# Two attention layers on one core: the last output block multiplied bank by bank, its last 72 rows prepared sooner

## The chip, the cores and the metric

The kernel runs on one core of a Trainium2 chip. The time is device microseconds of one execution. A core has a matrix engine (TensorE, PE in the profile, with its weight loads as PEld), three engines for element-wise work (VectorE or DVE, ScalarE or ACT, GpSimd or POOL), and SyncE (SP), which here issues nearly all of the transfers between DRAM and on-chip memory. On-chip memory is SBUF; the matrix engine writes into PSUM, eight banks of 128 partitions by 512 floats.

## The reference, cut to what matters

Two attention layers, A and B, work on two inputs of 2048 rows by 576 columns with 32 heads of 18. Their outputs stand side by side in the result. Only A matters for the change:

```python
q = (x @ wq).reshape(B, S, H, Dh).transpose(0, 2, 1, 3)   # 32 heads of 18
k = x @ wk                                                # one head, shared
v = x @ wv
p = softmax(einsum("bhqd,bkd->bhqk", q, k) * Dh ** -0.5)
o = einsum("bhqk,bkd->bhqd", p, v)
out_A = o.transpose(0, 2, 1, 3).reshape(B, S, H * Dh) @ wo
```

B is a causal attention in four segments with a memory that is carried from segment to segment. The last lines of the work, and the whole change, belong to the product with `wo` of A.

## The kernel before, in words

The 2048 rows of each layer are worked in four chunks (`c`) of 512 columns of a transposed layout: heads and their 18 features lie on partitions, rows of x lie along the free axis. A block is (layer, chunk, group of four heads); the list `blocks` mixes those of A and B, and the last one is chunk 3 of A, head group `hg` 7. Blocks are cut into turns `k` of three score tiles. In each turn of the main loop (L1130) the kernel writes the scores for this turn (PE), their exponentials (ACT, some by DVE), and the products with the values for the turn two before (`products`, L919). The engines PE, ACT and DVE run their instructions in the order in which the program writes them. SP and POOL get an order from a scheduler, which works from dependencies and its own cost estimates; the order of the text is only one input of that.

When a group of four heads is done, `products` copies its accumulator `O` to `oe` on DVE (L945) and stores it to the DRAM tensor `oA` (L947). Row 0 of each head's 19 rows is the sum of the softmax, rows 1 to 18 are the head's output. So the division comes later, in `finish` (L1005), as steps that are put into a list by `at` with a turn at which they are due, and taken from it by `due`:

- `begin` loads the sums from `oA` into `sm` (L674);
- `inv` takes the reciprocal on DVE (L688), stores it to `rA` (L695), and asks for the heads;
- `load` reads the heads' rows from `oA` into the tile `xh` (L702), 126 rows (seven heads) for each of t = 0 to 3, and 72 rows (four heads) for t = 4;
- `weights` reads the reciprocals, spread over the rows, into `rb` (L709);
- `heads` multiplies `xh` by `rb` on POOL (L723), which is called weighing.

Head group 6 of a chunk releases t = 0 to 3, head group 7 releases t = 4. For the last chunk the reciprocal of group 7 is due five turns after its `begin`.

Most chunks are multiplied with `wo` in the shade of later attention work, by `out_proj` (L752), which `run_fill` (L822) takes piece by piece into each turn. Two chunks are left for the end: chunks 2 and 3 of A, called `rows`. Their product is made differently: each operand is split into two float32r parts, a rounded one (`hi`, a copy on ACT, L1080) and the rest (`lo`, a subtraction on DVE, L1081). `halve_w(t)` does this for `wo`, `halve_heads(key, t)` for the heads. For t = 0 to 3 three matmuls then make one product. For t = 4 the 72 rows are repeated on more partitions with three transfers inside SBUF (`repeat`, L1108 to L1110), so that two matmuls do it; the halves of t = 4 are made by two casts on ACT (L1099) and two operations on DVE (L1100). `multiply` (L1198) runs over the eight PSUM banks for one t: four blocks of 128 output rows by two halves of 288 columns.

The end (from L1215) is written in this order: for chunk 2 the halves of t = 0 to 4 of weights and heads; then for chunk 3 the halves of t = 0 to 3, each after its weighing; then for each of the two chunks five calls of `multiply`, t by t over all eight banks, and four times two evictions (one on ACT, one on DVE, L1248) and a store of 128 rows (L750). For chunk 3, the transfers of `repeat` and the halves of t = 4 come just before the fifth `multiply`.

Of the kernel before, what the change touches and what calls it, by code (L numbers as in the profile page):

```python
# [8 lines left out]
F32 = mybir.dt.float32  # L9
F32R = mybir.dt.float32r  # L10
# [10 lines left out]
S, D, H, DH = 2048, 576, 32, 18  # L21
NSEG, L = 4, 512
C = 512
NCH = S // C
# [9 lines left out]
PBUFS = 9  # L34
# [43 lines left out]
def attention_pair_kernel(ctx, tc, a_xT, a_w, a_wo, b_xT, b_w, b_wo, b_beta, ident_d, hmask_d, bmask_d, cmask_d, sel_d, zmask_d, selx_d, sely_d, out):  # L78
# [840 lines left out]
    def products(b, m, hf):  # L919


        ab, c, hg = b
        if m == hf == 0:
            acc[0] = psO.tile([128, C], F32, name="O")
        o = acc[0]
        last = (NKT - 1 if ab == "A" else 2) == m
        for j in range(4):
            kt = turn_of(c, hg)[j // 2][m] if ab == "A" else m
            p = state[b + (kt,), j // 2]
            assert all(x[3] is not p for x in slow)  # L930
# [5 lines left out]
            nc.tensor.matmul(  # L936
                o[32 * j : 32 * j + 32, q0 : q0 + n],
                v,
                p[:, j % 2, p0 : p0 + n],
                start=m == hf == 0,  # L940
                stop=last and hf == 1,
            )
        if last and hf:
            osb = pa.tile([128, C], F32, name="oe", bufs=4)
            nc.vector.tensor_copy(osb, o)  # L945
            od = oA if ab == "A" else oB
            nc.sync.dma_start(od[c][4 * hg : 4 * hg + 4].rearrange("h r t -> (h r) t"), osb)  # L947
            return hg
        return None

# [29 lines left out]
    next(memory)  # L980
    prefetch("A", 2)
    FILL = 60
    later, weighed, loaded, summing = [], {}, [0], set()
# [21 lines left out]
    def finish(k, ab, c, hg):  # L1005

        ts = range(4) if hg == 6 else range(4, 5)
        lo, hi = (0, 28) if hg == 6 else (28, 32)
        box, need = {}, 3 if ab == "B" and c > 0 else 1
        weighed.setdefault((ab, c), 0)  # L1010
        last = (ab, c) == blocks[-1][:2]

        d0, d1, d2, d3 = (0, 2 if hg == 6 else 5, 0, 3) if last else (2, 5, 3, 5) if (ab, c) == ("B", 0) else (2, 4 if ab == "B" and hg == 6 else 5, 3, 6)

        def begin(k):
            assert ab == "A" or c not in LATE_ASK or asked[0] >= c
            summing.add(hg)
            box[0] = sums(ab, c, lo, hi)
            at(k + d1, 0, lambda: True, inv)

        def inv(k, part=0, of=1 if last or hg == 7 else 4 if ab == "B" and c else 2):
            inverses(ab, c, lo, hi, box[0], part, of)
            if part < of - 1:
                at(k + 1, 0, lambda: True, lambda k: inv(k, part + 1, of))
                return
            summing.remove(hg)
            for t in ts:
                at(k, 0, place, lambda k, t=t: load(k, t))
# [12 lines left out]

        def weights(k, t):
            loaded[0] += need
            tiles = load_inverses(ab, c, t)
            box[t, t] = weigh(ab, c, t, tiles)
            at(k + d3, 1, lambda: True, lambda k: heads(k, t))

        def heads(k, t):
            box[t, t].pop(0)()
            if box[t, t]:  # L1050
                at(k, 1, lambda: True, lambda k: heads(k, t))
                return
# [14 lines left out]
    with tc.manual_schedule(engines={ENG.PE, ENG.Activation, ENG.DVE}):  # L1067
# [59 lines left out]
            nc.vector.tensor_reduce(fms[0:1, 1:2], pf[0:1, 0:128], axis=AX.X, op=ALU.max)  # L1127

        wparts = []
        for k in range(len(turns) + 2):  # L1130
            now[0] = k
            exps = [scores(its[n], pr, i == 1) for i, (n, pr) in enumerate(turns[k])] if k < len(turns) else []
# [16 lines left out]
            ends = k > 1 and any(hf and its[n][3] == (NKT - 1 if its[n][0] == "A" else 2) for n, hf in prods[k - 2])  # L1149
            if slow and (slow[0][0] <= k or not ends):  # L1150
# [30 lines left out]
                fill.pop(0)  # L1181
            k += 1

        rows = [key for key, steps in fill] + [blocks[-1][:2]]
        assert len(rows) == 2 and all(ab == "A" for ab, c in rows)
        halves_of = {}

        def halve_heads(key, t):
            R = RT[t]
            x = halves_of[key, t] = pp.tile([128, 2, 512], F32R, name="P", bufs=PBUFS)  # L1190
            if t < 4:
                halve(x[:R, 0], x[:R, 1], parts[key][:R, t])
                return
            hi = pp.tile([128, 2, 512], F32R, name="PD", bufs=2)
            mixed(x[:, 0], hi[:, 0], parts[key][:, 4], some[:, 0:1])
            mixed(x[:88, 1], hi[:88, 1], raws[key], some[:88, 1:2])

        def multiply(key, t, dst):  # L1198
            R = RT[t]
            x = halves_of[key, t]  # L1200
            for g in range(8):
                i, c0 = g // 2, 288 * (g % 2)
                for m, (xp, wp) in enumerate(((0, 0), (1, 0), (0, 1)) if t < 4 else ((0, 0), (1, 1))):
                    if t == 4:
                        R = (128, 88)[m]
                    nc.tensor.matmul(
                        dst[g],
                        x[:R, xp, 128 * i : 128 * i + 128],
                        wparts[wp][:R, t, c0 : c0 + 288],
                        start=t == m == 0,  # L1210
                        stop=t == 4 and m == 1,
                    )


        repeat(rows[0])  # L1215
        for t in range(5):
            if t:
                halve_w(t)
            due(k, 4)
            k += 1  # L1220
            halve_heads(rows[0], t)
        for t in range(4):
            while weighed[rows[1]] <= t:
                due(k, 4)
                k += 1
            halve_heads(rows[1], t)
        for n, key in enumerate(rows):
            end = key == rows[-1]
            banks = [psE.tile([128, 2, 512], F32, name="E") for _ in range(3)]
            dst = [bk[:, hf, :288] for bk in banks for hf in range(2)]  # L1230
            dst += [psO.tile([128, C], F32, name=nm)[:, :288] for nm in ("O", "F")]
            for t in range(5):
                while end and weighed[key] <= t:
                    due(k, 4)
                    k += 1
                if end and t == 4:
                    repeat(key)
                    halve_heads(key, t)
                multiply(key, t, dst)
            for i in range(4):  # L1240
                if end:
                    osb = pp.tile([128, 2, 512], F32, name="P", bufs=PBUFS)[:, :, :288]
                elif i < 2:
                    osb = pp.tile([128, 2, 512], F32, name="W", bufs=2)[:, :, :288]
                else:
                    osb = pa.tile([128, D], F32, name="osb", bufs=2).rearrange("p (f n) -> p f n", f=2)
                for hf in range(2):
                    (nc.vector.tensor_copy if hf else nc.scalar.copy)(osb[:, hf], dst[2 * i + hf])  # L1248
                out_store(*key, i, osb)
        assert not later  # L1250
    attention.close()

# [226 lines left out]
```

## Time and profile before

| what | value |
|---|---|
| median of three runs | 1404.8 us (1403.82 to 1405.02) |
| the profiled execution's own time | 1405.02 us |
| its span, first to last instruction | 1403.3 us |
| PE busy | 1383.7 us, 99% of the span |
| ACT busy | 1199.0 us, 85% |
| DVE busy | 1048.5 us, 75% |
| POOL busy | 233.2 us, 17% |
| DMA moved | 173.67 MB, mean 124 GB/s |

The span is what the profile shows of the execution; the time of a run is a little longer, since it holds what lies around the program. Rows of a timeline begin with the start in us from the start of the span and the length; then engine, line of the kernel, operation, tile written and tiles read, sizes, and count; an idle time before it stands in brackets with what ended it. Where SP carries a q (SPq), the row is the issuing of a transfer, not the transfer itself. The length of several merged instructions reaches from the first start to the last end.

### The profile page before, as it was taken

What the parts mean: (1) busy time and instruction counts of PE and PEld (TensorE: products, weight loads), DVE (VectorE), ACT (ScalarE), POOL (GpSimd) and SP (SyncE); (2) the same over time, 40 slices, a digit from 0 to 9 for tenths busy, and PEclk for the clock granted to TensorE, in tenths of its full rate; (3) what the DMA queues carried; (4) which work ended last, traced back from release to release, by engine and by line L of the source; (5) the groups of instructions that cost most, each with busy time, mean ns of one, the idle gap of its engine ahead of it and who ended that gap; (6) DMA issues with size and microseconds to landing.
All of it is one profiled execution on the core that took longest, in us unless ns stands there. A gap on an engine that the chain in (4) does not pass through costs nothing.

```text
span 1403.3 us, 41194 instructions
## 1 busy us (share of the span) xinstructions
PE 1383.7 (99%) x17452; PEld 836.5 (60%) x17452; DVE 1048.5 (75%) x1565; ACT 1199.0 (85%) x1484; POOL 233.2 (17%) x342
## 2 busy tenths in 40 slices
PE   9999999999999999999999999999999999999997
PEld 6787888755554555555555555555555555555557
DVE  6656466477787788787888877876878778887884
ACT  4543434489999999999999999999999999999991
POOL 2442000003312211412110122113010220001002
PEclk9999999999999999999999999999999999999999
DMA  9866546577465445332312442232103221110023
GB/s 273 264 213 188 160 144 227 177 221 217 141 192 168 137 144 165 99 116 78 112 59 71 144 155 60 86 118 80 52 34 102 100 76 47 35 61 21 18 83 112
DMA packets 91288, 173.67 MB, mean 124 GB/s; under 512 B 14702, under 2 KB 23015, under 8 KB 90668
## 3 DMA queue, kind: packets, MB, share of 16 engines
q1 hardware_dynamic: 84968, 161.24, 36.8%
q0 software_dynamic: 1664, 4.78, 1.3%
q10 hardware_dynamic: 4464, 4.93, 1.0%
q8 instruction: 139, 2.28, 0.7%
q14 instruction: 53, 0.43, 0.1%
HBM read 99.65 MB, written 70.67 MB: 121 GB/s over the span
## 4 chain that ended last, share of the span: by engine, by line


## 5 line engine op out<-in xcount | busy, mean ns | idle before, releaser
L906 ACT ACTIVATE P<-E 128x1024 f32<-128x1024 f32 (+1 forms) x800 | 787.5, 1075 | 2.1 <-PE E L888 1.6
L903 DVE COPY W<-E 128x1024 f32<-128x1024 f32 (+2 forms) x416 | 453.3, 1090 | 142.9 <-PE E L888 80.5
L936 PE MATMUL O<-P,VA 128*32 128x256 f32 x7504 | 507.1, 379 | 0.0
L906 ACT ACTIVATE P<-W 128x1024 f32<-128x1024 f32 (+1 forms) x330 | 370.0, 1121 | 6.3 <-DVE W L903 5.7
L936 PEld LDWEIGHTS O<-P,VA 128*32 128x32 f32 x7504 | 259.1, 110 | 137.7 <-issue 4.3
L888 PE MATMUL E<-xl,kstA 56*128 56x512 f32 x1920 | 317.3, 430 | 2.0 <-ACT P L906 1.8
L888 PEld LDWEIGHTS E<-xl,kstA 56*128 56x128 f32 x1920 | 155.0, 184 | 159.1 <-issue 96.1
L911 POOL TENSOR_SCALAR_AFFINE_SELECT P<-P 128x256 f32<-128x256 f32 (+1 forms) x192 | 94.6, 493 | 410.0 <-ACT P L906 401.4
L723 POOL TENSOR_TENSOR xh<-xh,rb 126x512 f32<-126x512 f32 (+1 forms) x55 | 70.7, 1308 | 432.7 <-DVE PD L869 185.0
L739 PE MATMUL F<-woB,xh 126*32 126x192 f32 (+1 forms) x1920 | 126.5, 338 | 0.0
L936 PE MATMUL O<-PD,VA 128*32 128x256 f32 x688 | 88.9, 379 | 0.0
L739 PEld LDWEIGHTS F<-woB,xh 126*32 126x32 f32 (+1 forms) x1920 | 38.6, 108 | 74.8 <-issue 68.7
L936 PE MATMUL O<-P,vseg 128*32 128x256 f32 (+2 forms) x1536 | 81.5, 344 | 0.1
L945 DVE COPY oe<-O 128x512 f32<-128x512 f32 x64 | 44.3, 692 | 42.8 <-PE O L936 42.5
L862 DVE TENSOR_SCALAR PD<-E 128x512 uint32<-128x512 f32 x86 | 59.2, 688 | 17.8 <-PE E L888 16.1
L259 PE MATMUL pj<-xh,wBh 128*126 128x512 f32 x180 | 72.1, 400 | 0.0
L259 PE MATMUL pj<-xh,wBl 128*126 128x512 f32 x180 | 71.6, 398 | 0.0
L124 ACT CAST qp<-pj 126x512 fp32r<-126x512 f32 (+1 forms) x54 | 30.8, 583 | 39.3 <-DVE kmB L454 22.4
L739 PE MATMUL F<-woA,xh 126*32 126x192 f32 (+1 forms) x960 | 63.9, 338 | 0.0
L896 PE MATMUL E<-stB 56*128 56x256 f32 (+3 forms) x512 | 61.4, 348 | 2.0 <-ACT P L906 1.5
L936 PEld LDWEIGHTS O<-P,vseg 128*32 128x32 f32 x1536 | 48.8, 109 | 24.4 <-issue 1.8
L125 DVE TENSOR_TENSOR qp<-pj,qp 126x512 fp32r<-126x512 f32 (+1 forms) x54 | 36.7, 685 | 35.6 <-ACT qp L124 35.6
(222 smaller groups left out, 1556.5 us busy)
## 6 DMA issues: line engine op xcount, KB each, us to landing
stB<-kB SPq DMA_DIRECT2D x96, 144.0 KB
stB<-qB SPq DMA_DIRECT2D x32, 288.0 KB
xl<-qA SPq DMA_DIRECT2D x30, 288.0 KB
oA<-oe SPq DMA_DIRECT2D x32, 256.0 KB
oB<-oe SPq DMA_DIRECT2D x32, 256.0 KB
qA<-qp SPq DMA_DIRECT2D x16, 504.0 KB
kB<-qp SPq DMA_DIRECT2D x16, 504.0 KB
qB<-qp SPq DMA_DIRECT2D x16, 504.0 KB
```

The lines of the kernel that those rows point to most:

```text
L125: hold(nc.vector.tensor_tensor(qp[:R, 1, :n], src, qp[:R, 0, :n].bitcast(F32), op=ALU.subtract))
L259: nc.tensor.matmul(dst, w[:, c0 : c0 + M], x, start=i == 0, stop=i == len(ops) - 1)
L723: ins = tc.keep_in_program_order(nc.gpsimd.tensor_tensor(dst, a, b, op=op))
L739: nc.tensor.matmul(dst[32 * j : 32 * j + 32], parts[ab, c][: RT[t], t, r0 : r0 + 32], wo[ab][: RT[t], t, c0 : c0 + n], start=start, stop=stop,
L862: v.tensor_scalar(y, e, EXP_A, EXP_B, op0=ALU.mult, op1=ALU.add)
L888: nc.tensor.matmul(e[:, j], kstA[rows, 128 * kt : 128 * kt + 128], st[rows, h, :], start=True, stop=True)
L896: nc.tensor.matmul(e[:, j, c0 : c0 + 512 - 128 * k], st[rows, 4 + h, ks], st[rows, h, 128 * k :], start=True, stop=True)
L903: gate.append(nc.vector.tensor_copy(src[:, hs, :n], e[:, hs, :n]))
L906: nc.scalar.activation(p[:, hs, :n], src[:, hs, :n], AF.Exp, scale=SCALE)
L911: nc.gpsimd.affine_select(diag, diag, pattern=[[0, 2], [0, m], [1, 128]], base=0, channel_multiplier=-1, compare_op=ALU.is_ge, fill=0.0)
L936: nc.tensor.matmul(o[32 * j : 32 * j + 32, q0 : q0 + n], v, p[:, j % 2, p0 : p0 + n], start=m == hf == 0, stop=last and hf == 1,)
L945: nc.vector.tensor_copy(osb, o)
```

## The change

Four things are done.

1. The store of `oe` of the very last block goes to ScalarE's DMA queue instead of SP's.
2. For the last chunk's head group 7, `inv` (reciprocal, store of `rA`, and then the load of the 72 rows, the read of `rb` and the weighing) isn't put into the list with a due turn, but held, and written right behind the halves of t = 3 of chunk 2. `repeat` for chunk 3 is written right after its weighing, ahead of all multiplications.
3. Chunk 2's halves of the heads for t = 0 and of the weights for t = 1 are written in the last turn of the main loop, on both sides of the last piece of `out_proj`, so ahead of the last `oe` copy.
4. The last chunk is multiplied bank by bank: for each of the eight banks all five t, then its eviction; a store follows each pair of banks, and the last 128 rows are stored in two halves. Its t = 4 halves are written behind chunk 2's evictions.

```diff
@@ products
-            nc.sync.dma_start(od[c][4 * hg : 4 * hg + 4].rearrange("h r t -> (h r) t"), osb)
+            queue = nc.scalar if b == blocks[-1] else nc.sync
+            queue.dma_start(od[c][4 * hg : 4 * hg + 4].rearrange("h r t -> (h r) t"), osb)
@@ finish, begin
-            at(k + d1, 0, lambda: True, inv)
+            if last and hg == 7:
+                held.append(inv)
+            else:
+                at(k + d1, 0, lambda: True, inv)
@@ main loop
+        first, second = ("A", NCH - 2), ("A", NCH - 1)
...
+            if k > len(turns):
+                halve_heads(first, 0)
             if memory is None:
                 whole = run_fill()
...
+            if k > len(turns):
+                halve_w(1)
@@ the end
-        repeat(rows[0])
+        repeat(first)
         for t in range(5):
-            if t:
+            if t > 1:
                 halve_w(t)
             due(k, 4)
             k += 1
-            halve_heads(rows[0], t)
+            if t:
+                halve_heads(first, t)
+            if t == 3:
+                held.pop()(k)
         for t in range(4):
-            while weighed[rows[1]] <= t:
+            while weighed[second] <= t:
                 due(k, 4)
                 k += 1
-            halve_heads(rows[1], t)
...
+            halve_heads(second, t)
+        while weighed[second] <= 4:
+            due(k, 4)
+            k += 1
+        repeat(second)
...
+        dst = eight_banks()
+        for t in range(5):
+            multiply(first, t, dst)
...
+        halve_heads(second, 4)
+        dst = eight_banks()
+        for i in range(4):
+            osb = pp.tile([128, 2, 512], F32, name="P", bufs=PBUFS)[:, :, :288]
+            for hf in range(2):
+                for t in range(5):
+                    multiply(second, t, dst, [2 * i + hf])
+                evict(osb, hf, dst[2 * i + hf])
+                if i == 3:
+                    r0 = second[1] * C + 128 * i
+                    nc.sync.dma_start(out[r0 : r0 + 128, 288 * hf : 288 * hf + 288], osb[:, hf])
+            if i < 3:
+                out_store(*second, i, osb)
```

`multiply` takes the banks as an argument (`gs`, all eight by default). `evict` is the copy of L1248, on DVE for the second bank of a pair and on ACT for the first; `eight_banks` names the same eight banks as before.

More of the change, by code (lines that the diff above doesn't have):

```diff
@@ L982, in attention_pair_kernel @@
     FILL = 60
-    later, weighed, loaded, summing = [], {}, [0], set()
+    later, weighed, loaded, summing, held = [], {}, [0], set(), []
     turns, prods = [], []
@@ L1129, in attention_pair_kernel, with halve_heads @@
         wparts = []
+        first, second = ("A", NCH - 2), ("A", NCH - 1)
+        halves_of = {}
+        def halve_heads(key, t):
+            R = RT[t]
+            x = halves_of[key, t] = pp.tile([128, 2, 512], F32R, name="P", bufs=PBUFS)
+            if t < 4:
+                halve(x[:R, 0], x[:R, 1], parts[key][:R, t])
+                return
+            hi = pp.tile([128, 2, 512], F32R, name="PD", bufs=2)
+            mixed(x[:, 0], hi[:, 0], parts[key][:, 4], some[:, 0:1])
+            mixed(x[:88, 1], hi[:88, 1], raws[key], some[:88, 1:2])
         for k in range(len(turns) + 2):
@@ L1182, in attention_pair_kernel, with multiply @@
             k += 1
[L1184 to L1198, printed above, removed]
+        assert [key for key, steps in fill] + [blocks[-1][:2]] == [first, second]
+        def multiply(key, t, dst, gs=range(8)):
             R = RT[t]
             x = halves_of[key, t]
-            for g in range(8):
+            for g in gs:
                 i, c0 = g // 2, 288 * (g % 2)
@@ L1220, in attention_pair_kernel @@
             k += 1
-            halve_heads(rows[0], t)
+            if t:
+                halve_heads(first, t)
+            if t == 3:
+                held.pop()(k)
         for t in range(4):
-            while weighed[rows[1]] <= t:
+            while weighed[second] <= t:
                 due(k, 4)
                 k += 1
-            halve_heads(rows[1], t)
-        for n, key in enumerate(rows):
-            end = key == rows[-1]
+            halve_heads(second, t)
+        while weighed[second] <= 4:
+            due(k, 4)
+            k += 1
@@ L1229, in attention_pair_kernel, with eight_banks @@
+        repeat(second)
+        def eight_banks():
             banks = [psE.tile([128, 2, 512], F32, name="E") for _ in range(3)]
             dst = [bk[:, hf, :288] for bk in banks for hf in range(2)]
[L1231 to L1249, printed above, removed]
+            return dst + [psO.tile([128, C], F32, name=nm)[:, :288] for nm in ("O", "F")]
@@ new lines, in evict @@
+        def evict(osb, hf, src):
+            (nc.vector.tensor_copy if hf else nc.scalar.copy)(osb[:, hf], src)
+        dst = eight_banks()
+        for t in range(5):
+            multiply(first, t, dst)
+        for i in range(4):
+            if i < 2:
+                osb = pp.tile([128, 2, 512], F32, name="W", bufs=2)[:, :, :288]
+            else:
+                osb = pa.tile([128, D], F32, name="osb", bufs=2).rearrange("p (f n) -> p f n", f=2)
+            for hf in range(2):
+                evict(osb, hf, dst[2 * i + hf])
+            out_store(*first, i, osb)
@@ new lines, in attention_pair_kernel @@
+        halve_heads(second, 4)
+        dst = eight_banks()
+        for i in range(4):
+            osb = pp.tile([128, 2, 512], F32, name="P", bufs=PBUFS)[:, :, :288]
+            for hf in range(2):
+                for t in range(5):
+                    multiply(second, t, dst, [2 * i + hf])
+                evict(osb, hf, dst[2 * i + hf])
+                if i == 3:
[3 more added lines that the diff above has]
+                out_store(*second, i, osb)
```

## The prediction

> **What bounds the kernel now.** I read the page first, then the last 40 us engine by engine.
>
> ```profile
> span 1403.3 us, 41194 instructions
> ...
> PE 1383.7 (99%) x17452; PEld 836.5 (60%) x17452; DVE 1048.5 (75%) x1565; ACT 1199.0 (85%) x1484; POOL 233.2 (17%) x342
> ```
>
> TensorE (PE) is busy for 99% of the span, so this kernel only gets shorter where PE idles or after its last matmul. The whole change lies behind the last attention products, at 1364. There the timeline of PE (start, length, line, tiles, count, idle before) has:
>
> ```profile
> 1364.11 0.40 PE L1206 MATMUL E<-stB,P 126*128 126x288 f32 x1
> 1365.60 2.53 PE L1206 MATMUL E<-stB,P 126*128 126x288 f32 x17 [1.08 <-DVE P L1081]
> ...
> 1368.76 2.56 PE L1206 MATMUL E<-stB,P 126*128 126x288 f32 x18
> ...
> 1371.96 2.56 PE L1206 MATMUL E<-stB,P 126*128 126x288 f32 x18
> ...
> 1378.36 1.77 PE L1206 MATMUL E<-stB,P 128*128 128x288 f32 x12
> ...
> 1380.51 2.55 PE L1206 MATMUL E<-stB,P 126*128 126x288 f32 x18
> ...
> 1393.30 1.77 PE L1206 MATMUL E<-stB,P 128*128 128x288 f32 x12
> ...
> 1395.18 0.43 PE L1206 MATMUL F<-stB,P 128*128 128x288 f32 x2
> ```
>
> Two blocks of 112 matmuls run here, 24 for each of t=0..3 and 16 for t=4 (the last 72 rows). From 1368.76 to 1371.96 is one round of 24: 3.20 us, 0.133 each; t=4 takes 1380.51 - 1378.36 = 2.15. The reader is to see three things. The second matmul should follow the first at 1364.24 and comes at 1365.60: 1.36 us are lost to a late VectorE (DVE) half. All else is dense up to 1395.18 + 0.43 = 1395.61. And t=4 of the second block is used as late as 1393.30. Now DVE and the queue of SP:
>
> ```profile
> 1360.74 0.75 DVE L1081 TENSOR_TENSOR stB<-woA,stB 126x576 fp32r<-126x576 f32 x1
> 1362.96 0.36 DVE L763 COPY osb<-F 128x192 f32<-128x192 f32 x1 [1.47 <-PE F L739]
> 1364.25 0.69 DVE L945 COPY oe<-O 128x512 f32<-128x512 f32 x1 [0.94 <-PE O L936]
> ...
> 1369.78 0.68 DVE L1081 TENSOR_TENSOR P<-xh,P 126x512 fp32r<-126x512 f32 x1
> 1370.38 1.55 DVE L1091 TENSOR_SCALAR stB<-woA 128x576 fp32r<-128x576 f32 x1
> 1371.84 0.81 DVE L1100 SCALAR_TENSOR_TENSOR stB<-W,some 88x576 fp32r<-88x576 f32 x1
> 1372.57 1.78 DVE L1100 SCALAR_TENSOR_TENSOR P<-PD,some,xh 128x512 fp32r<-128x512 f32 x1
> ...
> 1377.78 0.24 DVE L688 RECIPROCAL sm<-sm 128x16 f32<-128x16 f32 x1
> ...
> 1392.33 0.74 DVE L1100 SCALAR_TENSOR_TENSOR P<-PD,some 88x512 fp32r<-88x512 f32 x1
> ...
> 1395.92 0.45 DVE L1248 COPY P<-F 128x288 f32<-128x288 f32 x1
> ```
> ```profile
> 1365.25 0.45 SPq L947 DMA_DIRECT2D oA<-oe  x1
> 1365.76 1.58 SPq L702 DMA_DIRECT2D xh<-oA  x2
> 1370.70 0.59 SPq L674 DMA_DIRECT2D sm<-oA  x1
> ...
> 1378.05 0.34 SPq L695 DMA_DIRECT2D rA<-sm  x1
> 1379.50 0.65 SPq L709 DMA_DIRECT2D rb<-rA  x1
> 1384.37 0.59 SPq L1108 DMA_DIRECT2D PD<-xh  x1
> 1385.01 1.09 SPq L750 DMA_DIRECT2D out<-W  x2
> ...
> 1387.19 0.82 SPq L1109 DMA_DIRECT2D PD<-xh  x1
> 1388.06 0.81 SPq L1110 DMA_DIRECT2D xh<-xh  x1
> 1394.95 2.40 SPq L750 DMA_DIRECT2D out<-P  x4
> ```
> ```profile
> 1383.07 1.28 POOL L723 TENSOR_TENSOR xh<-xh,rb 72x512 f32<-72x512 f32 x1 [7.56 <-DMA rb<-rA]
> ```
> ```profile
> 1391.01 0.62 ACT L1099 CAST PD<-xh 128x512 fp32r<-128x512 f32 x1 [10.14 <-DMA xh<-xh]
> ```
>
> This is the chain for the last 72 rows: store of oe, read of the sums (sm), reciprocal, store of rA, broadcast read of rb, weighing on POOL, three copies (L1108 to L1110), then the halves of t=4, done at 1392.33 + 0.74 = 1393.07. PE wants them at 1393.30. Only because all other products of the block come first is this chain hidden, with 0.23 us to spare.
>
> **The change, part by part.**
>
> *First halves sooner: -1.36.* The two subtractions (0.68 and 0.75) move from behind the oe copy to ahead of it. One goes into the 1.47 us that DVE idled before 1362.96, the other between that copy's end, 1363.32, and 1364.25, where it leaves 0.18. If it doesn't fit, the oe copy, and all behind it, slips by what is missing. PE then runs on from 1364.11.
>
> *The oe store on ScalarE's queue: 0.* ACT stands at it until the oe copy ends, 1364.94, and issues for about 0.45 (SP's row for the same store). Behind it wait ACT's copies for t=1 and on. The t=1 copy (0.62, as ACT's row) ends at 1366.0 and DVE subtracts until 1366.7; PE gets to t=1 at 1364.11 + 3.20 = 1367.31, which is the cover: 0.6 us. For DVE the halves of t=1 to 3 come when they came before, the last ending at 1369.78 + 0.68 = 1370.46. What the store gains is on SP:
>
> ```profile
> SPq L674 <- DMA oA<-oe: 3.3, 1, 3.3
> ```
>
> SP waited 3.3 us for its landing, until 1370.70, 5.45 after the issue, with reads of heads in the same queue. No row shows it on a queue of its own: I bound its landing by the small write of rA (1379.50 - 1378.05 = 1.45, so 1366.4) and by what it is now. I take 1368, near the middle.
>
> *The reciprocal behind t=3 of the first block: the decisive term.* DVE is free for it at 1370.46, not at 1377.78. But it needs sm, and sm must get through SP's DMA queue. The stretches there (busy times, clock, DMA share, GB/s):
>
> ```profile
> 1367.50:1373.00 5.50, 5.50 (x43) 5.50 (x42) 5.50 (x6) 1.24 (x2) 3.69 (x3) 1.00 0.46 177
> 1373.00:1373.50 0.50, 0.50 (x6) 0.50 (x5) 0.50 (x1) 0.00 (x0) 0.50 (x1) 1.00 0.33 56
> ```
>
> The sizes, from the list of DMA issues:
>
> ```profile
> sm<-oA SPq DMA_DIRECT2D x1, 8.0 KB
> ```
> ```profile
> rb<-rA SPq DMA_DIRECT2D x1, 144.0 KB
> ```
>
> The reads of heads run at 177 GB/s on 0.46 of the engines up to 1373.0; the slow, small packets that look like sm come only then. rb moves 144 KB and is used 3.57 after its issue, yet sm, 8 KB, issued at 1370.70, still had not moved 2.3 us on. So an earlier issue at 1368 finds the same reads in front of it, and sm lands at about 1373.8 (the stretch's end plus my estimate of 0.3). Bounds: 1370.46, if it may pass them, and 1374.3. I take 1373.8, since the rows show it last.
>
> [...]
>
> From sm to t=4, all by rows: reciprocal to rA's issue 0.27, to rb 1.45, to POOL 3.57, to the copies 1.30: 6.59. L1108 to the next issue 0.64 and L1109 to L1110 0.87: 1.51. L1110 to ACT 2.95 in the trace, but with four stores of a block in the same queue; 1.45 is rA's; I take the middle, 2.2. ACT's start to the second DVE half 1393.07 - 1391.01 = 2.06. Together 12.36: t=4 is ready at 1386.2 (1385.4 to 1387.4 by the bounds of the landing and of sm held up).
>
> Meanwhile DVE stands at the reciprocal from 1370.46 to 1374.0; behind it are four operations for t=4 of the first block, 1.55, 0.81, and two of 1.78 beside POOL or 0.74 without: 1377.9 (to 1380.0). PE wants them at 1364.11 + 4 x 3.20 = 1376.9, so it waits about 1.0. Then four subtractions and the first eviction follow, and the second block starts near 1380.9.
>
> *The last block bank by bank.* Each bank now needs t=4 after 12 matmuls: at 1382.5 at the latest, not at 1393.30. PE waits 3.7 us, until 1386.2. Then come 2 + 7 x 14 = 100 matmuls less the one that the first half lets through, 13.3 us, plus 0.17 until the last ends: 1399.6. The small wait before lies inside this: the chain alone sets the end.
>
> *The stores between: -0.5.* Now the last of four stores ends at 1394.95 + 2.40 = 1397.35, 1.74 after the last matmul. After: the copy starts 0.31 behind the matmul (1395.92 - 1395.61), 0.45, issue 0.45: 1.21. What follows on SP is:
>
> ```profile
> SPq L1254 <- SPq L1254: 3.6, 1, 3.6
> ```
>
> This 3.6 is put to SP's own branch, not to a landing, so I keep it and what follows. The tail goes from 7.69 to 7.16. Were the landing the limit, I estimate 1.5 saved instead: of the burst of four stores, half a store would be left.
>
> **Sum:** 1399.6 + 7.16 = 1406.8 against 1403.3, so +3.5. The profiled execution took 1405.02, its span and 1.72 around it; it is the slowest of three, 0.2 over the median. 1404.8 + 3.5 = 1408.3. Own range 1406.5 to 1410.0.
>
> **Rivals.**
>
> *The clock drops in the new gap.* The stretches after the last matmul:
>
> ```profile
> 1400.00:1400.50 0.50, 0.00 (x0) 0.00 (x0) 0.00 (x0) 0.00 (x0) 0.00 (x0) 0.65 0.08 25
> 1400.50:1403.00 2.50, 0.00 (x0) 0.00 (x0) 0.00 (x0) 0.00 (x0) 0.00 (x0) 0.50 0.03 8
> ```
>
> A mean of 0.65 there is full clock until 1400.15, 4.5 us after the last matmul, then half. A gap of 3.7 is shorter, so this speaks against; but it is one case. If recovery takes as long, half of 4.5 us is lost: 1408.3 + 2.3 = 1410.6.
> [...]
>
> *SP sends the first block's four stores ahead of the three copies.* It did so between L1108 and L1109 (1385.01 to 1387.19). Against it: the copies are now written ahead of those stores. Price: 2.2 us of issue and 0.75 of the longer landing: 1411.2.
>
> *sm isn't held up*, and the change does what it says. The reciprocal is at 1370.46, t=4 ready at 1382.8, PE done at 1396.2, span 1403.4: not slower, 1404.9; with the faster landing and the shorter tail 1403.2. For it: only SP's order and an inference from rates speak for the hold-up.
>
> *Faster by more than 0.2%.* PE would have to end by 1393.3 (or 1394.3 with the shorter tail), so t=4 be ready by 1380.9: 1.9 us sooner than even the free chain. Then bubble and tail together give up to 2.9: 1401.9. No row supports so short a chain.
>
> **Chances.** Forecast 0.47, clock 0.11, stores ahead 0.11, sm free 0.25, faster 0.06. 0.2% is 2.8 us, about what a measurement here can tell from no change. Slower: 0.47 x 0.95 + 0.22 = 0.67; same: 0.25 + 0.02 = 0.27; faster 0.06. The range reaches from the low end of the free chain, 1403.2, to 1411.6, past the stores' case.
>
> **What would show it.** PE dense from 1364.11 shows the first term; a DVE wait of some 3 us at L688 for sm shows the hold-up; a PE wait on the t=4 halves inside the second block's first bank shows the third; the last store 1.2 after the last matmul the fourth. I am wrong if sm lands before 1371, or if PE does not stop in that bank.

## The result and the profile after

| | kernel before | kernel after |
|---|---|---|
| median | 1403.96 us | 1411.42 us |
| lowest to highest of six | 1403.82 to 1405.02 | 1410.99 to 1413.22 |
| span of the profiled execution | 1403.3 us | 1409.4 us |

The ratio is 1.0054, 95% interval 1.0041 to 1.0067: slower by 7.5 us. Beside later kernels the changed one was timed once more, at 1.0046 (1.0032 to 1.0060).

One thing has to be set right before the traces are compared. In the profiled execution of before the first `oe` copy starts at 318.99 us, in that of after at 317.13, and most of that distance, 1.75 of 1.86 us, is still there at the end of the attention work. The edits come a thousand microseconds later; executions of all kernels here differ like that in their first 317 us: the first `oe` copy lies between 317.06 and 319.04. So the traces are laid one over the other at the first output matmul, 1364.11 in before and 1362.36 in after. Counted from there to the end of the span, before takes 39.19 us and after 47.04: 7.85 us more, near the 7.5 us of the medians. (Spans are given to 0.1 us, so sums with the end of the span are good to 0.05.)

Where they went is seen on PE. The timeline of PE in the changed kernel (start, length, line, tiles, count, idle before and who ended it):

```profile
1362.36 2.66 PE L1217 MATMUL E<-stB,P 126*128 126x288 f32 x18
...
1375.26 0.30 PE L1217 MATMUL E<-stB,P 128*128 128x288 f32 x1
1375.71 1.75 PE L1217 MATMUL E<-stB,P 88*128 88x288 f32 x11 [0.16 <-DVE P L1104]
...
1377.57 0.43 PE L1217 MATMUL F<-stB,P 128*128 128x288 f32 x2
1378.49 1.85 PE L1217 MATMUL E<-stB,P 126*128 126x288 f32 x12 [0.49 <-DVE W L1252]
1384.98 1.27 PE L1217 MATMUL E<-stB,P 128*128 128x288 f32 x2 [4.64 <-DVE P L1104]
1386.74 5.94 PE L1217 MATMUL E<-stB,P 126*128 126x288 f32 x28 [0.49 <-ACT P L1252]
1393.17 3.97 PE L1217 MATMUL E<-stB,P 126*128 126x288 f32 x28 [0.49 <-ACT P L1252]
1397.63 2.13 PE L1217 MATMUL E<-stB,P 126*128 126x288 f32 x14 [0.49 <-ACT P L1252]
1399.60 2.01 PE L1217 MATMUL O<-stB,P 126*128 126x288 f32 x14
1401.44 2.03 PE L1217 MATMUL F<-stB,P 126*128 126x288 f32 x14
```

The bubble behind the first output matmul is gone. The second block starts 0.65 us later than it would without a wait for DVE's eviction, runs the first bank's twelve matmuls of t = 0 to 3, and stops for the halves of t = 4. Then come two things to look at: 28 matmuls take 5.94 us in one row and 3.97 in the next, and before each second bank of a pair PE stands for ScalarE's eviction. The stretches of the changed kernel (busy times of PE, PEld, DVE, ACT, POOL, then the granted clock, DMA share, GB/s):

```profile
1384.30:1384.40 0.10, 0.00 (x0) 0.00 (x0) 0.10 (x1) 0.10 (x1) 0.00 (x0) 0.63 1.25 461
...
1391.10:1391.20 0.10, 0.10 (x3) 0.10 (x1) 0.00 (x0) 0.00 (x0) 0.00 (x0) 0.73 0.00 0
```

A stretch that the edge of the clock falls into has a mean between 0.5 and 1, and the mean tells where: the clock goes to half at 1384.33, inside PE's stop, and comes back at 1391.15. This is the chain that PE waits for, first DVE, then the issuing of transfers on SP and ScalarE, POOL, and ScalarE's cast:

```profile
1366.86 1.79 DVE L1085 TENSOR_TENSOR P<-xh,P 126x512 fp32r<-126x512 f32 x1
1372.12 0.25 DVE L688 RECIPROCAL sm<-sm 128x16 f32<-128x16 f32 x1 [3.47 <-DMA sm<-oA]
...
1384.85 0.74 DVE L1104 SCALAR_TENSOR_TENSOR P<-PD,some 88x512 fp32r<-88x512 f32 x1
```
```profile
1362.56 2.44 SPq L702 DMA_DIRECT2D xh<-oA  x3
1369.15 0.58 SPq L674 DMA_DIRECT2D sm<-oA  x1
...
1372.40 0.36 SPq L695 DMA_DIRECT2D rA<-sm  x1
1374.14 0.65 SPq L709 DMA_DIRECT2D rb<-rA  x1
1379.23 0.59 SPq L1112 DMA_DIRECT2D PD<-xh  x1
1379.87 0.82 SPq L1113 DMA_DIRECT2D PD<-xh  x1
1380.73 0.80 SPq L1114 DMA_DIRECT2D xh<-xh  x1
...
1402.07 2.27 SPq L1275 DMA_DIRECT2D out<-P  x2
```
```profile
1363.22 0.34 ACTq L948 DMA_DIRECT2D oA<-oe  x1
...
1383.53 0.62 ACT L1103 CAST PD<-xh 128x512 fp32r<-128x512 f32 x1 [5.33 <-DMA xh<-xh]
```
```profile
1377.64 1.56 POOL L723 TENSOR_TENSOR xh<-xh,rb 72x512 f32<-72x512 f32 x1 [4.34 <-DMA rb<-rA]
```

DVE stands at the reciprocal for 3.47 us, until the sums have landed; the halves of t = 4 end at 1385.59. That is 23.2 us after the first output matmul, where before it was 29.0 (1393.07 - 1364.11). So the change does bring the 72 rows sooner, by 5.7 us. But it wants them 11.5 us sooner: 17.7 us after the first output matmul (1380.09), where before it was 29.2 (1393.30).

**An account of the 7.85 us**, from these rows:

| step | us |
|---|---|
| bubble behind the first output matmul gone | -1.36 |
| t = 4 of the first block: 1375.71 instead of 1375.40 | +0.31 |
| second block starts at 1378.49 instead of 1377.84, for DVE's eviction | +0.65 |
| stop for t = 4: 1384.98 instead of 1378.49 + 12 x 0.133 = 1380.09 | +4.89 |
| its second half later still, by PEld's idle time | +0.37 |
| three waits for ScalarE's eviction, 0.72 each, 0.81 the first | +2.25 |
| half clock: 1403.47 against 1398.49, less the two lines above | +2.36 |
| after the last matmul: 1409.4 - 1403.47 = 5.93 instead of 7.69 | -1.76 |
| sum | 7.71 |

1398.49 is 1384.98, 100 matmuls of 0.133 us at full clock, and 0.17 until the last ends. The half clock's line is what is left of PE's time, not a count of its own; 0.14 of the 7.85 us stay without a line. Each larger line is a theory of its own; the experiments take them one by one.

### The profile page after: what moved, and what is told of

It is laid out like the page before. It is cut to its first block, busy times and chain, and to the rows that moved or that the text cites. A ratio compares the mean times of both kernels' runs of the same rounds, so it can differ in the third digit from the quotient of the medians.

```text
span 1409.4 us, 41198 instructions
## 1 busy us (share of the span) xinstructions
PE 1385.6 (98%) x17452; PEld 837.0 (59%) x17452; DVE 1045.1 (74%) x1565; ACT 1199.9 (85%) x1484; POOL 233.2 (17%) x342
```

## The experiments

The theories: (1) PE's stop for t = 4 carries most of the loss, and it is the order of the banks that makes it; (2) the half clock comes from that stop and costs over 2 us more; (3) the three waits come from the two banks of a pair lying in one tile; (4) the sums are late because the big reads of heads are ahead of them. The rivals are named with each run. Ratios are to the kernel before, run on the same chip beside them. The table gives, from the profiled execution, PE's time from the first output matmul's start to the last one's end, the rest of the span, and their sum. The changed kernel and its repeat differ by 0.4 us in the sum, so a difference of that size between two traces says nothing.

| kernel | PE | rest | sum | median, ratio (95%) |
|---|---|---|---|---|
| before | 31.50 | 7.69 | 39.19 | 1 |
| after | 41.11 | 5.93 | 47.04 | 1411.42, 1.0054 (1.0041 to 1.0067) |
| t by t | 31.39 | 7.53 | 38.92 | 1404.96, 0.9996 (0.9987 to 1.0005) |
| pairs | 39.44 | 6.19 | 45.63 | 1409.75, 1.0034 (1.0021 to 1.0048) |
| busy gap | 39.41 | 6.04 | 45.45 | 1411.71, 1.0050 (1.0037 to 1.0064) |
| halves only | 30.65 | 7.82 | 38.47 | 1402.66, 0.9984 (0.9975 to 0.9993) |
| sums first | 45.29 | 6.13 | 51.42 | 1416.39, 1.0084 (1.0070 to 1.0098) |
| store on SP | 40.85 | 6.00 | 46.85 | 1412.60, 1.0062 (1.0049 to 1.0076) |
| banks only | 46.90 | 5.80 | 52.70 | 1416.87, one run |
| six banks | 30.14 | 6.01 | 36.15 | 1400.57, 0.9975 (0.9964 to 0.9985) |
| after, again | 41.40 | 6.05 | 47.45 | 1411.10, 1.0046 (1.0032 to 1.0060) |
| pairs and busy gap | 37.06 | 6.16 | 43.22 | 1408.67, 1.0028 (1.0017 to 1.0039) |
| six banks, store on SP | 30.12 | 5.91 | 36.03 | 1400.29, 0.9972 (0.9963 to 0.9981) |

### Is it the order of the banks? (e1_t_by_t)

```diff
         halve_heads(second, 4)
         dst = eight_banks()
+        for t in range(5):
+            multiply(second, t, dst)
         for i in range(4):
...
             for hf in range(2):
-                for t in range(5):
-                    multiply(second, t, dst, [2 * i + hf])
                 evict(osb, hf, dst[2 * i + hf])
```

> The changed kernel, but the last block is multiplied t by t over all eight banks again, with its evictions behind; everything else of the change stays. If the loss is the order of the banks: t=4 is wanted some 12.8 us after the block's start (about 1391 in the changed kernel's trace) and was ready at 1385.6, so PE doesn't stop, the clock stays full, and the end is 8 us sooner than in the changed kernel: 1403.3, a little under the kernel before (ratio about 0.9995). If the loss is in the other parts (ScalarE waiting at the store, the reciprocal in VectorE's way): it stays above 1408.

Measured: 0.9996. PE in this kernel:

```profile
1379.27 2.66 PE L1217 MATMUL E<-stB,P 126*128 126x288 f32 x18 [0.49 <-DVE W L1252]
...
1394.04 0.43 PE L1217 MATMUL F<-stB,P 128*128 128x288 f32 x2
```

No stop, no wait behind the start of the second block. All the other parts of the change are in it, so the loss hangs on the order of the banks. The rest of the span is 7.53, nearly that of before, though the last 128 rows are stored in two halves here too: the shorter end of the changed kernel belongs to its spread-out stores, not to the halved one.

### The bank order alone (e7_banks_only)

```diff
-                multiply(key, t, dst)
+                if not end:
+                    multiply(key, t, dst)
...
                 for hf in range(2):
+                    for t in range(5) if end else ():
+                        multiply(key, t, dst, [2 * i + hf])
                     (nc.vector.tensor_copy if hf else nc.scalar.copy)(osb[:, hf], dst[2 * i + hf])
```

This is the kernel before; the last store in halves is added too.

> The kernel before, with only the last block multiplied bank by bank and its last rows stored in halves. The 72 rows are ready at 1393.1 there, 11 us after the first bank wants them: PE stops that long, the clock drops, three pair waits of 0.7: span about 1417, time about 1418. If the stop hides in something else: 1411 or less.

Measured: span 1415.2, one time of 1416.87. PE:

```profile
1378.90 1.74 PE L1206 MATMUL E<-stB,P 126*128 126x288 f32 x12
1391.08 1.27 PE L1206 MATMUL E<-stB,P 128*128 128x288 f32 x2 [10.44 <-DVE P L1100]
```

The stop is 10.4 us where the changed kernel has 4.6. Together with the run before: the sooner chain is worth 5.8 us of the stop, and the bank order costs more than that.

### The two banks of a pair (e2_pairs)

```diff
-            for hf in range(2):
-                for t in range(5):
-                    multiply(second, t, dst, [2 * i + hf])
+            for g in (2 * i, 2 * i + 1) if i < 3 else ():
+                for t in range(5):
+                    multiply(second, t, dst, [g])
+            for hf in range(2):
+                for t in range(5) if i == 3 else ():
+                    multiply(second, t, dst, [2 * i + hf])
                 evict(osb, hf, dst[2 * i + hf])
```

> The changed kernel, but for the first three pairs of banks both banks are multiplied before either is evicted. If the three waits of PE for ScalarE's eviction come from the two banks sharing one tile, they go, 0.72 us each, 2.2 together: 1409.2. If PE would have stood there anyway (slow weights, the clock): 1411.4 as before. The stop for t=4 and the clock drop stay in either case.

Measured: 1409.75, 1.0034. The waits are gone; one row runs through all three pairs:

```profile
1385.89 12.30 PE L1217 MATMUL E<-stB,P 128*128 128x288 f32 x72 [5.35 <-DVE P L1104]
```

PE takes 39.44 instead of 41.11, 1.67 less, where 2.2 were expected; t = 4 came 0.8 us later in this execution (1385.89 - 1362.47 = 23.42, against 22.62). The program holds matmuls into one bank back until ScalarE has copied the other bank of the same tile, 0.72 to 0.81 us of PE a pair in the changed kernel and none here: in `eight_banks` the first six banks are three tiles of two banks, and a wait goes by tile. The last pair, O and F, are tiles of their own and had no wait in the changed kernel either.

### The clock (e3_busy_gap)

```diff
                 for t in range(5):
+                    if i == hf == 0 and t == 4:
+                        for _ in range(36):
+                            nc.tensor.matmul(dst[7], halves_of[second, 0][:126, 0, :128],
+                                wparts[0][:126, 0, :288], start=True, stop=True)
                     multiply(second, t, dst, [2 * i + hf])
```

> The changed kernel with 36 matmuls whose result is not used (into the last bank, which is started afresh later) put into the gap before the first bank's t=4: 36 x 0.133 = 4.8 us of a gap of 4.89. If the gap makes the clock drop and that costs 2.4 us by itself: no half clock in the records and 1409.0. If only the stop counts and the slow stretch is something else: 1411.4. If the extra matmuls are in the way: above 1411.4.

Measured: 1411.71, 1.0050. In the trace the clock does what the theory says. PE, and a stretch behind the gap:

```profile
1382.11 4.90 PE L1273 MATMUL F<-stB,P 126*128 126x288 f32 x36
1387.18 0.40 PE L1217 MATMUL E<-stB,P 128*128 128x288 f32 x1 [0.18 <-DVE P L1104]
```
```profile
1387.18:1392.00 4.82, 4.07 (x26) 3.64 (x27) 1.07 (x2) 0.40 (x1) 0.00 (x0) 1.00 0.19 72
```

Full clock throughout, and PE takes 39.41 instead of 41.11, 1.70 less, though t = 4 was ready 0.4 us later here. The time shows no gain: 1409.0 was expected, and all five runs lie above 1411.2. In this execution the first `oe` copy is at 319.04, that of the changed kernel at 317.13, so what was won at the end was lost before the first 319 us, where no edit is. That alone doesn't decide it, so the edit was run again with another.

### Both small edits together (e10_pairs_busy, after_again)

The diffs are those of the two runs before, the 36 matmuls ahead of the first bank's t = 4.

> The changed kernel once more, beside the two that follow, so that they can be compared on one chip: 1411.4, 1.0054 of the kernel before.

> The changed kernel with both small edits: pairs of banks before their evictions, and 36 matmuls without use in the gap. By the traces of the two edits alone (1.7 and 1.7 us less from the first output matmul to the last) both together take 3.4 us off if they are independent: 1408.0 against 1411.4. If the clock drop costs nothing in the time, as its run alone looked: 1409.7.

Measured: 1.0046 and 1.0028; 1411.10 and 1408.67, 2.4 us apart. PE 41.40 and 37.06. To leave out when t = 4 came, PE can be counted from its first matmul of t = 4 in the second block to its last: 18.49 us in the changed kernel and 16.38 with the busy gap, 16.02 with the pairs and 14.08 with both. So at full clock that stretch is 2.1 and 1.9 us shorter, and the clock's loss is real in the traces; by the times, taken together with the pairs, the two edits are worth 2.4 us of the 3.4 expected, and the intervals (1.0032 to 1.0060, 1.0017 to 1.0039) just overlap. The pairs alone would explain 1.7 of it. The half clock's 2 us are shown by the traces and not by the times.

### What the sums wait for (e5_sums_first, e6_store_sp)

In the first, the reads of heads of the last chunk stand behind the read of the sums on SP:

```diff
         def place():
+            if last and hg == 6 and not sums_read:
+                return False
...
         def load(k, t):
-            load_heads(ab, c, t)
+            ld = load_heads(ab, c, t)
+            if last and t < 4:
+                tc.add_manual_dep(ld.ins, sums_read[0].ins.name, AFTER, reason="behind the sums")
```

> The changed kernel, but SP issues the four big reads of heads of the last chunk behind the read of the sums. If those reads hold up the store's landing and the sums: both land some 3.5 us sooner (reciprocal right behind the halves of t=3, where it had stood 3.5 us), t=4 is ready 3.5 us sooner, PE stops about 2 us instead of 5.3, and a gap that short leaves the clock at full: 1405.5. If store and sums take their time by themselves: the reciprocal is where it was and the time stays at 1411.4, or is worse, since the heads then come later.

In the second, only the queue is undone:

```diff
-            queue = nc.scalar if b == blocks[-1] else nc.sync
+            queue = nc.sync
```

> The changed kernel with the last oe store on SP's queue again. In the changed kernel it landed 5.9 us after its issue on ScalarE's queue, against 5.4 on SP's in the kernel before. If the queue doesn't matter: 1411.4 within 1, reciprocal within 0.5 us of where it was. If ScalarE's queue did bring the store ahead of the reads: the reciprocal is 1 to 2 us later and the time 1412.5 to 1413.5. If the wait on ScalarE cost something: below 1411.

Measured: 1.0084 and 1.0062. The first, on SP and DVE:

```profile
1369.53 0.61 SPq L674 DMA_DIRECT2D sm<-oA  x1
1370.23 4.67 SPq L702 DMA_DIRECT2D xh<-oA  x5
1375.01 0.63 SPq L695 DMA_DIRECT2D rA<-sm  x1
1381.50 0.67 SPq L710 DMA_DIRECT2D rb<-rA  x1
```
```profile
1371.70 0.25 DVE L688 RECIPROCAL sm<-sm 128x16 f32<-128x16 f32 x1 [1.04 <-DMA sm<-oA]
...
1379.28 5.41 DVE L1094 TENSOR_TENSOR P<-xh,P 126x512 fp32r<-126x512 f32 x4 [4.97 <-ACT P L1093]
```
```profile
1385.12 3.25 PE L1226 MATMUL E<-stB,P 126*128 126x288 f32 x12 [4.44 <-DVE W L1261]
1392.68 1.26 PE L1226 MATMUL E<-stB,P 128*128 128x288 f32 x2 [4.31 <-DVE P L1113]
```

Its first output matmul is at 1365.48 and its `oe` store is issued at 1366.34. From that issue to the reciprocal it takes 5.4 us (1371.70); in the changed kernel 8.9 (1363.22 to 1372.12). The 3.5 us that were expected are there, in two parts: the store's landing, seen by the issue of the sums' read, 3.2 instead of 5.9, and the sums, 2.2 instead of 3.0. So theory (4) holds, but the larger part of the wait is the store's: the sums are read late because the store of `oe` lands late, and are then held 0.8 us more. But the loss is larger than the gain. The reads are now ahead of the store of `rA`, and from its issue to that of `rb` it takes 6.5 us instead of 1.7; and the heads themselves are late, so that DVE's subtractions end at 1384.7 and PE stops twice, for 4.4 and 4.3 us. The hold-up was moved, not removed. That a stop of about 2 us leaves the clock at full was the author's estimate, and this run doesn't test it, since the stops were longer; in the run with the halves alone the clock fell 1.64 us after the last matmul.

Why the store lands late can be read from the packets of its queue: the store is all that q10, ScalarE's queue, carries here (256 KB in 144 packets), and q1 is SP's. Packets that moved:

| run, stretch | SP's queue | the store |
|---|---|---|
| after, 1364.0 to 1365.5 | 100 | 79 |
| after, 1365.5 to 1366.9 | 129 | 2 |
| after, 1366.9 to 1368.7 | 107 | 63 |
| sums first, 1367.0 to 1368.0 | 4 | 135 |

With the reads, over half of the store moves at once, then it all but stands for 1.4 us while the reads move, and the rest follows by 1368.7; the sums' read is issued at 1369.15. Without them 135 of the 144 packets move within one microsecond, in which the DMA moves 255 GB/s. So it is the store's data that waits, not only the news of its end.

The second, SP and DVE:

```profile
1363.59 0.71 SPq L948 DMA_DIRECT2D oA<-oe  x1
1364.35 1.58 SPq L702 DMA_DIRECT2D xh<-oA  x2
1369.12 0.59 SPq L674 DMA_DIRECT2D sm<-oA  x1
```
```profile
1372.16 0.25 DVE L688 RECIPROCAL sm<-sm 128x16 f32<-128x16 f32 x1 [5.74 <-DMA sm<-oA]
```

From the first output matmul (1362.45) to the reciprocal it is 9.7 us, in the changed kernel 9.8. On SP's queue the store lands 5.5 us after its issue, on ScalarE's 5.9, with reads of heads issued just ahead of it and just behind it in both. The other queue brought nothing. Its median is above the changed kernel's, but the intervals overlap, and the sum in the trace is 0.2 lower, less than the two traces of the changed kernel differ by.

### The first halves alone (e4_halves_only)

```diff
+            if k > len(turns):
+                halve_heads(("A", NCH - 2), 0)
             if memory is None:
                 whole = run_fill()
...
+            if k > len(turns):
+                halve_w(1)
```

This is the kernel before, with the two halves taken out of the later loop.

> The kernel before, with only the first halves moved into the last turn of the main loop. If the bubble behind the first output matmul was worth its 1.36 us: 1402.6 (ratio 0.9990), PE dense from the first output matmul on. If the moved subtractions push the oe copy or the copy of the last fill back by as much: 1404.0.

Measured: 1402.66, 0.9984. PE:

```profile
1364.03 2.65 PE L1210 MATMUL E<-stB,P 126*128 126x288 f32 x18
...
1392.39 1.75 PE L1210 MATMUL E<-stB,P 88*128 88x288 f32 x11 [0.24 <-DVE P L1100]
```

The bubble is gone, but PE takes 30.65 instead of 31.50, 0.85 less and not 1.36: with PE sooner, the second half of t = 4 of the last block isn't ready when PE comes to it, and PE stands for 0.4 us (1392.39 instead of 1391.85 + 0.13, by the row ahead of it). The time is consistent with the expected ratio of 0.9990.

### A version from the account (e8_six_banks, e11_six_banks_sp)

```diff
+        for t in range(4):
+            multiply(second, t, dst, range(6))
         for i in range(4):
...
+            gs = (2 * i, 2 * i + 1)
+            if i < 3:
+                for g in gs:
+                    for t in range(4 if g < 6 else 0, 5):
+                        multiply(second, t, dst, [g])
             for hf in range(2):
-                for t in range(5):
-                    multiply(second, t, dst, [2 * i + hf])
+                if i == 3:
+                    for t in range(4 if gs[hf] < 6 else 0, 5):
+                        multiply(second, t, dst, [gs[hf]])
                 evict(osb, hf, dst[2 * i + hf])
```

The reciprocal moves from behind t = 3 to behind t = 4 of the first block, and the first block's first pair is evicted by ScalarE alone, so that the second block doesn't wait for DVE there.

> A version to beat both: the changed kernel, but the last block runs t=0 to 3 for six banks first (9.6 us), then t=4 of these, pair by pair with evictions and stores between, then the last two banks whole; the reciprocal stands behind the halves of t=4 of the block before, and that block's first pair is evicted by ScalarE alone. If the trace is read rightly, t=4 is ready before it is wanted, PE stays dense (30.2 us from the first output matmul to the last, against 31.5 before), and the end is 5.9 after the last matmul against 7.7: 3.0 under the kernel before, ratio 0.9979. If the evictions between cost PE waits, or the shorter end belongs to the late stores alone: ratio 0.999 to 1.000.

> The six-banks version with the last oe store on SP's queue. If that queue doesn't matter: the same as the six-banks version, ratio 0.9975 to the kernel before within 0.001. If ScalarE's queue was worth something: 0.998 or more.

Measured: 0.9975 and 0.9972. Of the first, two stretches (from the first output matmul to the last, then to the end) and the second of DVE's halves of t = 4:

```profile
1362.05:1392.19 30.14, 30.14 (x228) 29.90 (x224) 17.09 (x23) 11.36 (x23) 8.12 (x5) 1.00 0.44 148
1392.19:1398.20 6.01, 0.00 (x0) 0.00 (x0) 0.46 (x1) 0.00 (x0) 0.00 (x0) 0.90 0.12 38
```
```profile
1385.50 0.74 DVE L1104 SCALAR_TENSOR_TENSOR P<-PD,some 88x512 fp32r<-88x512 f32 x1
```

PE is busy for all of its 30.14 us, at full clock. The halves of t = 4 are ready at 1386.24; PE wants them at 1386.71, 72 matmuls of t = 0 to 3 after the block's start at 1377.11, so the cover has half a microsecond to spare. The end takes 6.01. That is 3.04 us under the kernel before by the trace, as expected. The six banks of t = 0 to 3 are the cover that t = 4 needs; the evictions and stores between the banks are what shortens the end. The queue of the store makes no difference here either.

## Why the prediction was right or wrong

The side was right, and the time lies in the stated range, but only just below its upper end of 1411.6, and above the forecast's own range (1406.5 to 1410.0); the move was 7.5 us where 3.5 were forecast. That it lies in the range is in part luck: the upper end was made for the four stores ahead of the copies, which did not happen. What came instead, by the account above, is the half clock (2.36) and the waits within a pair (2.25), less 1.2 that the end gained beyond the forecast; the other terms came out 0.8 us above their forecast. Step by step, each counted from the first output matmul:

- *First halves sooner, -1.36*: right; the changed kernel has no bubble. That by itself the gain is smaller in the kernel before (0.85) was not seen: the 0.23 us of reserve at t = 4 of the last block, which the prediction read, are used up by it.
- *The oe store on ScalarE's queue, 0*: right for the path. The landing was taken at 1368, 3 us after the issue; it took 5.9, so this size was off by 2.9. A queue of its own was no help: with reads about it the store lands 5.5 us after its issue on one queue and 5.9 on the other.
- *The reciprocal behind t = 3, with sm held up by the reads*: right in its time and in its cause, wrong in its parts, so that the agreement is in part luck. sm was set at 1373.8, which is 9.7 us after the first output matmul; the reciprocal starts 9.76 after it. But the read of sm was to be issued at 1368, 3.9 after it, and held for 5.8; it was issued at 6.79, no sooner than in the kernel before (1370.70 - 1364.11 = 6.59), and took 2.97. The hold-up lies mostly in the store's landing. The experiment with the sums first shows the reads to be the cause of both parts, 2.7 and 0.8 us. Whether a read of sm issued sooner behind those reads would have been held for 5.8 us, no run shows. The rival in which the sums come early falls.
- *The rest of the chain, 12.36*: it took 13.47 (1372.12 to 1385.59). The landing of the three copies was taken as the middle, 2.2, and measured 2.80, near the upper bound; rA's landing took 1.74 instead of 1.45, POOL 1.56 instead of 1.28.
- *The stop in the first bank, 3.7*: the mechanism was right, its size 4.89 and another 0.37. One microsecond is the longer chain; the second block also started 0.7 us sooner than thought, since the wait for t = 4 of the first block was 0.31 instead of 1.0.
- *The clock drops in the new gap*: held as a rival with 0.11, at 2.3 us. It happened; the account gives 2.36, the traces of the experiments 1.9 and 2.1. What failed is the condition: "4.5 us after the last matmul" was read as the time that it takes, from one case, and 3.7 as shorter than that. In the traces the clock fell 1.64 to 4.84 us after the last matmul, and 2.52 to 4.33 us after the start of a stop, so a gap of 3.7 was no protection. And the recovery, taken as 4.5 us, was 6.83 (1384.33 to 1391.15).
- *The waits within a pair*: not foreseen at all, 2.25. In before each eviction is written behind all matmuls of the block, so that no row could show that a wait goes by tile and not by bank; the code shows the tile of two banks.
- *The stores between, -0.5*: measured -1.76, near the alternative that the prediction priced at 1.5. From the last matmul to the end of the last store's issue it took 0.87 instead of 1.74, and from there to the end 5.06 instead of 5.95; the 3.6 us that were put to SP's branch are 2.8 in the changed kernel, so they are not fixed. That the landing is the limit, as the alternative had it, is not shown: the last packet of the stores ends 3.3 us behind the last issue in before and 1.1 in after, and of these 2.2 us only 0.9 arrive at the end of the span.
- *The stores ahead of the copies*: did not happen; L1112 to L1114 stand ahead of the first block's four stores.

## What to carry to other kernels

An order of banks that ends early for each bank also wants every operand early: before reordering, look up when the last operand is ready, and put as much other work in front as that takes; six banks of t = 0 to 3 did it here, and then the stores between the banks paid 1.7 us at the end. Look also at what big reads are under way when a transfer on the critical chain is issued: here its store landed 5.9 us after its issue beside them, though it went to another engine's queue, and 3.2 without them; and putting the read of the sums ahead of them only made the next small one wait, 6.5 us from `rA` to `rb` instead of 1.7. And where tiles hold two banks and a wait goes by tile, don't evict one while the other is still to be written: it cost 0.72 to 0.81 us a pair here.

## What the runs showed of the hardware

The granted clock stood at 1.00 or at 0.50 in the stretches read here, and the lengths between its edges are multiples of one length. The half stretches before the end of the work last 6.83 us in the changed kernel (1384.326 to 1391.153), in its repeat, with the pairs and with the store on SP, and 13.65 with the sums first and with the banks alone: two and four times 3.41. The full stretches behind them fit the same length: 17.07 us in the changed kernel (1391.15 to 1408.22) is five times, and 13.65 with the pairs is four times. That the clock can change only every 3.41 us is the author's estimate from these lengths.

No one length of a stop set the drop. Behind the last matmul of the kernel the clock fell after 4.54 us in before and 4.75 in the changed kernel, but after 2.65 with the pairs, 2.18 in the second six-banks run and 1.64 in the run with the halves alone. In the last of these PE was still at work for 1.8 of the 3.41 us that ended with the fall; in before it was at work for 2.29 us of the stretch from 6.83 to 3.41 us ahead of the fall (1393.32 to 1396.74), and the clock was full until 1400.15. By the same estimate, when the clock falls depends on where a stop lies in these stretches. In all six executions in which PE stopped for 4.4 us or more between the first output matmul and the last, the clock dropped in the stop, 2.52 us after its start with the banks alone, 3.99 in the changed kernel, 4.33 in its repeat.

The landing of a write on one queue was held up by reads on another: a store of 256 KB landed 5.9 us after its issue with four reads of 252 KB issued on SP between 1361.2 and 1365.0, and 3.2 without them. The packets show where the time went: the store's last packet moved shortly before 1368.7, and the read that waits for it was issued 0.5 us later; in the run with the sums first the DMA moves 26 GB/s from 1368 to 1369 and nothing in the microsecond after it, and the read is issued at 1369.53. So what came late was the data, which shared the DMA engines with the reads: of their time SP's queue and the store took 46.2% and 0.4% from 1365.5 to 1366.9, and 29.4% and 16.6% from 1366.9 to 1368.7, 46% together in both.
